# Attention of all heads by pairs in float32: scores on row halves, values on column halves, and the weights turned by VectorE and moved by DMA

## The chip, the cores and the metric

The kernel runs on one core of a Trainium2 chip. The metric is the device time of one execution, in microseconds. The core has TensorE (PE in the profile, its weight loads PEld), VectorE (DVE), ScalarE (ACT), GpSimd (POOL) and the queue of SyncE (SP), which issues nearly all DMAs here.

## What is computed

Attention over 8 batches x 8 heads, 576 positions of 64 values each, with a mask in blocks of 64; then a feed-forward layer over the 4608 tokens of width 512, with a hidden width of 2048. Inputs and outputs are float32 (the weights of the feed-forward arrive as 64-bit floats).

```python
scores = (q @ k.T) / sqrt(64)                 # per head, 576 x 576
scores = where(i // 64 >= j // 64, scores, -1e9)
attn = exp(scores - scores.max(-1)); attn /= attn.sum(-1) + 1e-9
x = concat_heads(attn @ v)                    # 4608 x 512
h = x @ w_in                                  # 4608 x 2048
out = (h * sigmoid(1.702 * h)) @ w_out        # 4608 x 512
```

## The kernel before

**Feed-forward.** The tokens are cut into 12 tiles of 384. A tile runs over 16 units, one for each 128 hidden columns. A unit is 12 matmuls of 384 columns into the PSUM tile `hp` (each factor is split in a rounded part and a remainder, `xh`/`xl` and `wih`/`wil`, and three products are summed), then tanh on ACT (L517), `g` on DVE (L518, it reads `hp`), the split into `gh` (ACT, L522) and `gl` (POOL, L81), and, one unit later, 9 matmuls of 512 columns into `acc0` to `acc2`. `hp` has one buffer: the 12 matmuls of a unit wait until DVE has made the `g` of the unit before, and only that unit's 9 `acc` matmuls of the one before stand between.

**Attention.** A head is worked in 5 chunks of query rows: chunk 0 has 64 rows, chunks 1 to 4 have 128, against 64, 192, 320, 448 and 576 keys (`width`). `score` makes the scores of a chunk into a PSUM bank and takes their largest on DVE (L313), the exponentials and their sums on ACT (L321), then scales the weights `e` by the reciprocal of the sum (L330 to L344). `fill` turns the weights by PE transposes in blocks of 128x128 against `ident` (L382) and copies them to SBUF (L386, L389); `av` multiplies them with `v`. The first 17 heads (`early`) load q and k row by row and turn them on PE, and multiply turned weights and values in float32 (`vn`). The other 47 load q and k in 32-wide slices, turn them in 32x32 blocks on DVE (L244, L248), split them and multiply by rounded part and remainder on all 128 rows (`q1`, `k1`, `q2`, `ph`, `pl`, `vs`, `vd`).

**Order.** PE runs in the order in which the program is written. `step(n)` gives the slots of a head from the strings in `ORDER`. Behind each slot the feed-forward is advanced to a share of its work that `TILES_BY` gives by position: nothing up to head 8.8, one tile from there to head 17, nine tiles over the other 48 heads, and the last two tiles after all attention. The 32 weight pieces (`weight_piece`, 64 DMAs) are converted along the way by `WEIGHTS_BY`, the last at head 15. The other engines' instructions are put in order by a scheduler within these limits. An engine works its instructions off in that order, and a waiting one holds those behind it.

**Turns of names.** `xr` holds the result of attention, turned, as a ring of two batches; `bank()` hands out PSUM banks in turn: `w0` to `w3`, and `acc0` to `acc2` as well while the first heads run.

## Time and profile before

| | |
|---|---|
| time, median of 3 runs | 1218.23 us (1216.92 to 1220.74) |
| the profiled execution | 1218.16 us, span of its instructions 1216.4 us |
| granted TensorE clock, mean | 0.994 |
| PE / PEld busy | 1188.4 us (98%) / 1063.9 us (87%) |
| DVE / ACT / POOL busy | 872.0 (72%) / 706.7 (58%) / 367.6 (30%) us |
| DMA | 78.62 MB in 223772 packets, 65 GB/s in the mean |
| chain that ended last | PE 87%, DVE 7%, ACT 2%, issue 2% |

In a row of the groups by line stand line, engine, operation, output<-inputs with their shapes, count, then busy us in all and the mean ns of one, and behind the second bar the engine's idle time before them. A float32 matmul leaves two records in the trace, one for each pass. In a row of the timeline stand start, length, engine, line and operation; rows of one kind are merged, with their count at the end. Matmuls are pipelined, so that their length says less than the distance between two starts.

### The profile page before, as it was taken

What the parts mean: (1) busy time and instruction counts of PE and PEld (TensorE: products, weight loads), DVE (VectorE), ACT (ScalarE), POOL (GpSimd) and SP (SyncE); (2) the same over time, 40 slices, a digit from 0 to 9 for tenths busy, and PEclk for the clock granted to TensorE, in tenths of its full rate; (3) what the DMA queues carried; (4) which work ended last, traced back from release to release, by engine and by line L of the source; (5) the groups of instructions that cost most, each with busy time, mean ns of one, the idle gap of its engine ahead of it and who ended that gap; (6) DMA issues with size and microseconds to landing.
All of it is one profiled execution on the core that took longest, in us unless ns stands there. A gap on an engine that the chain in (4) does not pass through costs nothing.

```text
span 1216.4 us, 20880 instructions
## 1 busy us (share of the span) xinstructions
PE 1188.4 (98%) x6860; PEld 1063.9 (87%) x6860; DVE 872.0 (72%) x2460; ACT 706.7 (58%) x1773; POOL 367.6 (30%) x496
## 2 busy tenths in 40 slices
PE   6899999999999999999999999999999999999998
PEld 5667887789999999999999999999999999999997
DVE  6997788777887888778888787878788788611111
ACT  6886666655665565656665665565575566432322
POOL 3554454421321312321322232232132231232321
PEclk8999999999999999999999999999999999999999
DMA  8653444422222231232132232222232231000000
GB/s 201 162 152 94 118 117 119 108 42 51 50 70 44 55 76 40 48 81 50 38 76 55 44 70 50 51 70 45 53 76 43 46 77 30 4 26 1 27 1 26
DMA packets 223772, 78.62 MB, mean 65 GB/s; under 512 B 198832, under 2 KB 204848, under 8 KB 223664
## 3 DMA queue, kind: packets, MB, share of 16 engines
q1 hardware_dynamic: 222480, 77.00, 27.0%
q8 instruction: 54, 0.88, 0.3%
q14 instruction: 54, 0.44, 0.1%
q10 hardware_dynamic: 1184, 0.30, 0.1%
HBM read 50.87 MB, written 9.44 MB: 50 GB/s over the span
## 4 chain that ended last, share of the span: by engine, by line
PE 87%; DVE 7%; ACT 2%; issue 2%; DMA 1%; POOL 1%; POOLq 0%; SPq 0%; DVEq 0%; ACTq 0%
PE hp L92 32%; PE acc L92 32%; PE bank L92 15%; PE bank L95 8%; DVE e L313 1%; DVE wm L171 1%; DVE wm L176 1%; ACT e L321 1%; DVE sm L330 1%; DVE wm L167 1%; DVE e L342 1%; DVE qk L286 1%; DMA wst<-in_moe_w_out_dram 0%; DMA qkr<-in_q_dram 0%; DVE xr L427 0%
## 5 line engine op out<-in xcount | busy, mean ns | idle before, releaser
L81 POOL TENSOR_TENSOR gl<-g,gh 128x384 fp32r<-128x384 f32 x192 | 197.2, 1027 | 599.5 <-ACT gh L522 521.7
L321 ACT ACTIVATE e<-e,mx 64x64 f32<-64x64 f32 (+4 forms) x320 | 180.0, 563 | 214.8 <-DVE mx L313 213.8
L92 PE MATMUL hp<-xh,wih 128*128 128x384 f32 x768 | 268.0, 349 | 2.4 <-ACT wih L180 1.9
L92 PE MATMUL hp<-xl,wih 128*128 128x384 f32 x768 | 259.6, 338 | 1.2 <-POOL sm L297 1.2
L92 PE MATMUL hp<-xh,wil 128*128 128x384 f32 x768 | 259.0, 337 | 0.9 <-POOL wil L81 0.9
L92 PE MATMUL acc<-woh,gh 128*128 128x512 f32 x576 | 237.0, 412 | 0.5 <-ACT woh L180 0.5
L92 PE MATMUL acc<-wol,gh 128*128 128x512 f32 x576 | 227.2, 395 | 0.6 <-POOL wol L81 0.6
L92 PE MATMUL acc<-woh,gl 128*128 128x512 f32 x576 | 226.7, 394 | 0.5 <-POOL gl L81 0.5
L518 DVE SCALAR_TENSOR_TENSOR g<-g,hp 128x384 f32<-128x384 f32 x192 | 105.3, 548 | 129.4 <-ACT g L517 128.3
L313 DVE CUSTOM_DVE_ANT_0 e<-bank,mask 64x64 f32<-64x64 f32 (+4 forms) x320 | 132.9, 420 | 69.3 <-PE bank L92 65.6
L517 ACT ACTIVATE g<-hp 128x384 f32<-128x384 f32 x192 | 93.9, 489 | 119.2 <-PE hp L92 115.9
L95 PE MATMUL bank<-ident,e 128*128 128x128 f32 x960 | 153.9, 280 | 8.1 <-DVE e L342 5.6
L92 PEld LDWEIGHTS hp<-xh,wih 128*128 128x128 f32 x768 | 144.6, 188 | 11.5 <-ACT wih L180 2.1
L92 PEld LDWEIGHTS hp<-xh,wil 128*128 128x128 f32 x768 | 144.9, 189 | 9.6 <-POOL wil L81 1.2
L92 PEld LDWEIGHTS hp<-xl,wih 128*128 128x128 f32 x768 | 144.3, 188 | 1.6 <-POOL sm L297 1.6
L390 DVE TENSOR_TENSOR pl<-bank,ph 128x512 fp32r<-128x512 f32 (+2 forms) x188 | 102.4, 562 | 56.7 <-ACT ph L389 56.6
L342 DVE TENSOR_SCALAR e<-e,sm 64x64 f32<-64x64 f32 (+2 forms) x260 | 137.2, 557 | 4.9
L92 PEld LDWEIGHTS acc<-wol,gh 128*128 128x128 f32 x576 | 108.3, 188 | 26.2 <-POOL wol L81 1.1
L95 PEld LDWEIGHTS bank<-ident,e 128*128 128x128 f32 x960 | 112.1, 142 | 21.1 <-DVE e L342 8.0
L522 ACT CAST gh<-g 128x384 fp32r<-128x384 f32 x192 | 97.6, 508 | 52.9 <-DVE g L518 52.2
L92 PE MATMUL bank<-qk 128*128 128x320 f32 (+4 forms) x384 | 118.3, 308 | 2.7 <-DVE qk L286 1.8
L92 PEld LDWEIGHTS acc<-woh,gh 128*128 128x128 f32 x576 | 108.7, 189 | 11.0 <-ACT woh L180 0.7
(68 smaller groups left out, 1845.4 us busy)
## 6 DMA issues: line engine op xcount, KB each, us to landing
qkd<-qkd SPq DMA_DIRECT2D x94, 144.0 KB, 2.3
out_dram<-osb SPq DMA_DIRECT2D x36, 256.0 KB, 2.1
qkd<-in_q_dram SPq DMA_DIRECT2D x94, 72.0 KB, 2.4
qkd<-in_k_dram SPq DMA_DIRECT2D x94, 72.0 KB, 2.2
vr<-in_v_dram SPq DMA_DIRECT2D x47, 128.0 KB, 2.4
wst<-in_moe_w_out_dram SPq DMA_DIRECT2D x18, 256.0 KB, 3.2
qkr<-in_q_dram SPq DMA_DIRECT2D x17, 256.0 KB, 3.4
xr<-in_moe_w_in_dram SPq DMA_DIRECT2D x16, 256.0 KB, 3.1
```

What stands on the lines that cost most here:

```text
L81: eng.tensor_tensor(out=out, in0=in0, in1=in1, op=ALU.subtract)
L92: return tc.keep_in_program_order(nc.tensor.matmul(**kw))
L95: return tc.keep_in_program_order(nc.tensor.transpose(**kw))
L167: nc.vector.tensor_scalar(out=m, in0=m, scalar1=3, scalar2=None, op0=ALU.logical_shift_left)
L171: nc.vector.scalar_tensor_tensor(out=y, in0=w[..., 1], scalar=0x80000000, in1=y, op0=ALU.bitwise_and, op1=ALU.bitwise_or,)
L313: nc.vector.tensor_tensor_reduce(out=e[0:m, lo:hi], in0=s[0:m, 0 : hi - lo], in1=mk, op0=ALU.add, op1=ALU.min, scale=-0.125, scalar=3e38 i ...
L321: nc.scalar.activation(out=e[0:m, 0:w], in_=e[0:m, 0:w], func=AF.Exp, scale=-1.0, bias=mx[0:m, i : i + 1], accum_out=sm[0:m, i : i + 1],)
L342: nc.vector.tensor_scalar(out=x, in0=x, scalar1=sc, scalar2=None, op0=ALU.mult)
L390: nc.vector.tensor_tensor(out=lo, in0=tp[:, 0:tot], in1=f(hi), op=ALU.subtract)
L517: nc.scalar.activation(out=g, in_=hp[:, 0:tt], func=AF.Tanh, scale=1.702)
L518: nc.vector.scalar_tensor_tensor(out=g, in0=g, scalar=1.0, in1=hp[:, 0:tt], op0=ALU.add, op1=ALU.mult)
L522: nc.scalar.copy(out=gh, in_=g)
```

## The change

Attention is worked in 32 pairs of heads (`NPAIR`), all in one way.

- **Loads.** 8 DMAs bring q and k of both heads in 32-wide slices, head 0 on partitions 0 to 63, head 1 on 64 to 127 (`raw`); two DVE transposes turn them (`prep`, now L210). 4 DMAs bring the values (`vp`). No split and no second copy of anything is made. `raw`, `qk`, `vp` have one buffer each.
- **Scores.** One float32 matmul per chunk and head (two in chunk 4, for 256 and 320 keys), over 64 rows of the array: head 0 on rows 0 to 63, head 1 on rows 64 to 127, one behind the other, each into its own bank.
- **Weights.** They are scaled as before (by POOL, but for chunk 4, and in the first pairs chunk 0, by DVE or ACT: `SCALE_ON`), then turned by DVE in 32x32 blocks into `tw` (L282, L287 of the changed kernel), and behind chunk 4 of a pair 16 DMAs (L294) bring the blocks to their places in `pw`. `tw` and `pw` have one buffer each, and `e` one for even chunks and one for odd ones.
- **Values.** Float32 matmuls of 64 output columns: head 0 writes partitions 0 to 63 of the bank, head 1 partitions 64 to 127, one behind the other; two ACT copies then bring both heads to `xr`.
- **Order.** `01`, `23` and `4` stand for the scores of these chunks of pair n, `V` for the values of pair n-1, `L` for turning q and k of pair n+1 and loading those of n+2; behind each slot the feed-forward advances as before.
- **Weight pieces** are converted in halves, each with a buffer of its own.

```diff
-    "S0+F2 S1+F3 F4 S2 A S3 S4 F1+S5 B",
+    "01 - 23 - V 4 L -",
+    "01 - - - 23 - - V - 4 - - L - - -",
+    "01 - - - 23 - - V - 4 - - L - - -",
...
-TILES_BY = ((8.8, 0), (17, 1), (65, -2))
+TILES_BY = ((9, 0), (17, 1), (65, -2))
...
+    NS = 14
+    SLOT = (None, 0, 1, 3, 6)
+    turned = sp.tile([P, 8 * NS - 4, 2, 32], F32, name="turned")
+    tw, pw = [
+        turned[:, x : x + 4 * NS].rearrange("p (b s) h c -> p b s h c", b=4) for x in (0, 4 * NS - 4)
+    ]
...
+    def score(n, chunks):
...
+        for i in chunks:
+            a, z = qrange(i)
+            w = width(i)
+            for lo, hi in ((0, w),) if w <= 512 else ((0, 256), (256, w)):
+                for hd in range(2):
+                    s = bank()
+                    r = slice(hd * D, hd * D + D)
+                    mm(
+                        out=s[0 : z - a, 0 : hi - lo], lhsT=qk[n][r, 0, a:z], rhs=qk[n][r, 1, lo:hi],
+                        start=True, stop=True,
+                    )
+                    todo.append((i, hd, lo, hi, s))
+        e = {}
+        for i, hd, lo, hi, s in todo:
+            e[i] = weigh(n, i, hd, lo, hi, s, e.get(i))
+        for i in chunks:
+            turn(n, i, e[i])
...
+    def turn(n, i, e):
...
+        on = SCALE_ON[phase(n)][i]
+        for hd in range(2):
...
+            if i:
+                nc.vector.transpose(
+                    out=tw[:, :, SLOT[i] : SLOT[i] + i, hd].rearrange("p b j c -> p j b c"),
+                    in_=e[:, hd, 0 : i * P],
+                )
+        r = slice(BLK, P) if i else slice(0, BLK)
+        nc.vector.transpose(
+            out=tw[r, 0:2, 9 + max(i, 1)].rearrange("p b h c -> p h b c"), in_=e[r, :, i * P : w]
+        )
+        if i == NCH - 1:
+            for kb in range(4):
+                for qb in range(4):
+                    ns = 10 if kb > 1 else NS if qb > 1 else 11
+                    nc.sync.dma_start(
+                        out=pw[kb * 32 : kb * 32 + 32, qb, 0:ns], in_=tw[qb * 32 : qb * 32 + 32, kb, 0:ns]
+                    )
+
+    def av(n):
...
+        for x, (bk, c, nn, j, w) in enumerate(todo):
+            for hd in range(2):
+                mm(
+                    out=bk[hd * D : hd * D + D, c : c + nn].rearrange("d (a c) -> d a c", c=32),
+                    lhsT=vp[:, hd, j], rhs=w[:, :, hd], start=x in (0, last + 1), stop=x >= last,
+                )
```

What this does to the order is shown at one place of the stage in which 24 pairs pass beside nine tiles: the end of a pair's scores. On PE, before, the last scores of a head (`bank<-qk_9253` with 256 columns is the first part of chunk 4) stand among pieces of a unit:

```order
L92 MATMUL hp<-xl,wih 128x384
L92 MATMUL bank<-qk_9253 128x256
L92 MATMUL bank<-qk_9253,q_9254 128x256
L92 MATMUL acc_8728<-woh,gh 128x512
L92 MATMUL acc_8728<-woh,gl 128x512
L92 MATMUL acc_8728<-wol,gh 128x512
```

Now all four matmuls of chunk 4, two for each part, stand between the `acc` matmuls of one unit and the `hp` matmuls of the next:

```order
L83 MATMUL acc_5945<-wol,gh 128x512
L83 MATMUL bank<-qk 128x256 x2
L83 MATMUL bank<-qk 128x320 x2
L83 MATMUL hp<-xh,wih 128x384
L83 MATMUL hp<-xh,wil 128x384
```

What moved: the scores of two heads stand as one piece, and no transposes follow them. On DVE, before, a `g` of the feed-forward (L518) stands between the two parts of chunk 4, ahead of its scaling (`e_88` is chunk 4):

```order
L313 ISA e_88,mx<-bank,mask 128x256
L313 ISA mx 128x1
L330 TENSOR_SCALAR sm<-sm 128x1
L518 SCALAR_TENSOR_TENSOR g<-g,hp 128x384
L333 RECIPROCAL sm<-sm 128x1
L342 TENSOR_SCALAR e_86<-e_86,sm 128x448
L313 ISA e_88,mx<-bank,mask,mx 128x320
L313 ISA mx 128x1
```

Now the next `g` (L403) stands behind the last maximum of chunk 4, a transpose of `prep`, the reciprocal, the scaling and the three transposes of the weights:

```order
L249 ISA e,mx<-bank,mask,mx 128x320
L249 ISA mx 128x1
L210 STREAM_TRANSPOSE qk<-raw 128x576
L268 TENSOR_SCALAR sm<-sm 128x2
L271 RECIPROCAL sm<-sm 128x2
L278 TENSOR_SCALAR e<-e,sm 128x576 x2
L282 STREAM_TRANSPOSE turned<-e 128x4x4x32 x2
L287 STREAM_TRANSPOSE turned<-e 64x2x2x32
L403 SCALAR_TENSOR_TENSOR g<-g,hp 128x384
```

What moved: that `g` belongs to the unit whose `hp` matmuls stand right behind chunk 4 on PE, and the unit after it waits for it.

More of the change, by code (lines that the diff above doesn't have):

```diff
@@ L174, in weight_piece @@
             )
-        for w, y in halves:
             nc.vector.scalar_tensor_tensor(
@@ L189, in convert, with heads @@
             conv["n"] += 1
[L192 removed]
+    raw, qk = {}, {}
+    def heads(n):
+        b, h = divmod(n, HP)
+        return [(hd, b, 2 * h + hd) for hd in range(2)]
     def load(n):
[L195 to L212 removed]
+        raw[n] = d2.tile([P, 2, S // 32, 32], F32, tag="raw", name="raw", bufs=1)
+        for x, src in enumerate((q, k)):
+            for hd, b, h in heads(n):
@@ new lines, in load_v @@
+    def load_v(n):
+        for hd, b, h in heads(n):
+            nc.sync.dma_start(
+                out=vp[:, hd, 0:QC], in_=v[b, h, 0 : QC * P].rearrange("(c p) d -> p c d", p=P)
+            )
+            nc.sync.dma_start(out=vp[0:BLK, hd, QC], in_=v[b, h, QC * P : S])
+    def prep(n):
+        qk[n] = d2.tile([P, 2, S], F32, tag="qk", name="qk", bufs=1)
+        for x in range(2):
+            nc.vector.transpose(out=qk[n][:, x], in_=raw[n][:, x].rearrange("p c d -> p (c d)"))
+        raw.pop(n)
@@ L303, in score @@
         w = width(i)
-        e = es[i]
-        s = bank()
-        for qq, st in ((q1, True), (q2, False)):
-            mm(
-                out=s[0:m, 0 : hi - lo], lhsT=qq[:, a:z], rhs=k1[:, lo:hi],
-                start=st, stop=not st,
-            )
+        if e is None:
+            e = d2.tile([P, 2, w], F32, tag=f"e{i % 2}", name="e", bufs=1)
         last = i > 0 and hi == w
@@ L449, in step, with item @@
-        for ci in range(6):
-            items[f"S{ci}"] = on(now, score, n, ci)
-        return [[items[y] for y in x.split("+")] for x in ORDER[phase(n)].split()]
+        now = n < NPAIR
+        def item(x):
+            if x == "V":
+                return (lambda: av(n - 1)) if n else None
+            if x == "L":
+                return (lambda: (prep(n + 1), load(n + 2) if n + 2 < NPAIR else None)) if n + 1 < NPAIR else None
+            return (lambda: score(n, [int(y) for y in x])) if now and x != "-" else None
@@ L454, in attention_moe_kernel @@
+        return [item(x) for x in ORDER[phase(n)].split()]
     done = {"split": 0}
```

323 lines of the change are left out of this document (72 added, 251 removed), and 2 rows, old and new, of the table ORDER.

## The prediction

> **What bounds the kernel now.** I read the page's first part, then busy time by stretches, then the timeline of PE and the groups by line and shape.
>
> ```profile
> PE 1188.4 (98%) x6860; PEld 1063.9 (87%) x6860; DVE 872.0 (72%) x2460; ACT 706.7 (58%) x1773; POOL 367.6 (30%) x496
> ```
>
> The same by stretches (us, PE, PEld, DVE, ACT, POOL busy, granted clock, DMA share, GB/s), cut at the first `hp`, at the end of head 15 and at the end of attention:
>
> ```profile
> 0.00:92.00 92.00, 76.06 (x457) 57.59 (x457) 78.27 (x275) 73.60 (x209) 42.99 (x66) 0.96 0.66 171
> 92.00:231.00 139.00, 132.15 (x740) 106.75 (x740) 106.53 (x319) 92.39 (x240) 71.03 (x72) 0.98 0.42 110
> 231.00:1073.00 842.00, 840.92 (x4975) 774.46 (x4974) 668.50 (x1834) 500.87 (x1246) 214.13 (x320) 1.00 0.25 54
> 1073.00:1216.40 143.40, 139.26 (x694) 125.10 (x692) 18.68 (x34) 39.84 (x80) 39.43 (x40) 1.00 0.05 17
> ```
>
> PE never rests in the third stretch: what the change is worth there is what it takes from PE, less any wait that it brings. The cuts come from these timeline rows:
>
> ```profile
> 92.29 0.42 PE L92 MATMUL hp<-xh,wih 128*128 128x384 f32 x1
> ...
> 231.23 0.37 ACT L427 COPY xr<-bank 64x256 f32<-64x256 f32 x1
> ```
>
> The third stretch holds 48 heads, 24 pairs at 842 / 24 = 35.1 us. The `hp` instructions in it are 1728 matmuls, 144 units, 6 a pair. What a unit costs alone is read after attention:
>
> ```profile
> 231.00:1073.00 842.00, 355.13 (x1728) 305.52 (x1728) 78.29 (x143) 70.22 (x144) 1.00 0.25 54
> ...
> 1100.00:1150.00 50.00, 50.00 (x253) 45.30 (x251) 6.46 (x12) 15.30 (x31) 16.04 (x16) 1.00 0.05 17
> ```
>
> 253 matmuls of 21 a unit in 50 us are 4.15 us a unit, so 6 units are 24.9 us, and attention, with all it does to PE's flow, costs 35.1 - 24.9 = 10.2 us a pair. That is the number to beat.
>
> **PE's part of a pair.** It removes everything in the 10.2 (30 transposes, split scores, split values, the joints between them) and adds float32 matmuls: per head 1600 columns of scores (64 + 192 + 320 + 448 + 576) and as many of values, 6400 a pair. The early heads of before show such matmuls:
>
> ```profile
> 128.50 0.40 PE L92 MATMUL acc<-wol,gh 128*128 128x512 f32 x1
> 128.83 2.09 PE L92 MATMUL bank<-ph,vn 128*64 128x256 f32 x10
> 130.85 0.50 PE L92 MATMUL acc<-woh,gh 128*128 128x512 f32 x1
> 131.19 0.39 PE L92 MATMUL acc<-woh,gl 128*128 128x512 f32 x1
> 131.41 0.39 PE L92 MATMUL acc<-wol,gh 128*128 128x512 f32 x1
> ```
>
> Five matmuls (3 x 256 + 192 + 64 = 1024 columns, ten records) take 130.85 - 128.83 = 2.02 us. An `acc` matmul starts 0.22 us after another (131.41 - 131.19), but 0.33 and 0.34 us pass where float32 of another shape begins or ends: 0.1 us for each change. Less two such changes (the last matmul has 64 rows), a column costs (2.02 - 0.2) / 1024 = 1.78 ns. The Trainium skill, TensorEngine Tiling (Array Packing), section Tiling Modes, says that changing the tiling mode drains TensorE, which speaks against a kernel that goes to and fro; the trace agrees with its 0.1 us. A pair has four pieces (01, 23, V, 4), eight changes, 0.8 us.
>
> One after the other, 6400 columns cost 11.4 us, with the changes 12.2. But the two heads' matmuls, issued side by side, share no rows of the array (scores) or no columns (values). Were they to run two at a time, the columns cost 5.7 us. They are issued pass by pass, both passes of head 0 before those of head 1, so at the seams a pass stands without partner; I put 1.0 us for that (an estimate: one pass of each of 64 to 448 columns at 0.89 ns). That gives 7.5 us. The bounds are 5.9 (no such seams, changes mostly hidden) and 12.2. No row of before has two matmuls on different halves, so nothing there decides between 7.5 and 12.2; I take 7.5, as the operands leave no reason to wait and PE already works its loads and matmuls at once (87% and 98% busy). The same page and section says that different tiles can execute LdWeights and Matmul in parallel; no run so far shows it. By it the sum is the one below, without it that of rival B.
>
> **The wait that it adds.** `hp` has one buffer, and PE waited for `g` practically never:
>
> ```profile
> L92 PE MATMUL hp<-xh,wih 128*128 128x384 f32 x768 | 268.0, 349 | 2.4 <-ACT wih L180 1.9 <-DVE g L518 0.5
> ```
>
> Now, once a pair, the `g` of the unit behind chunk 4 stands on DVE behind chunk 4's whole softmax and turning. PE needs it one unit, 4.15 us, after chunk 4. The durations of that chain, from the groups by shape:
>
> ```profile
> L313 DVE CUSTOM_DVE_ANT_0 e<-bank,mask,mx 128x320 f32<-128x320 f32 x64 | 35.1, 549 | 11.4 <-PE bank L92 10.9
> L321 ACT ACTIVATE e<-e,mx 128x576 f32<-128x576 f32 x64 | 49.8, 777 | 5.2 <-DVE mx L313 5.0
> L321 ACT ACTIVATION_READ_ACCUMULATOR e<-e,mx 128x1 f32 x256 | 48.0, 188 | 0.0
> L330 DVE TENSOR_SCALAR sm<-sm 128x1 f32<-128x1 f32 x128 | 18.8, 147 | 5.2 <-ACT e L321 5.0
> L342 DVE TENSOR_SCALAR e<-e,sm 128x576 f32<-128x576 f32 x56 | 29.6, 529 | 1.6
> L244 DVE STREAM_TRANSPOSE tmp<-qkd 128x576 f32<-128x576 f32 x47 | 36.0, 765 | 0.5 <-DVE sm L330 0.4
> L518 DVE SCALAR_TENSOR_TENSOR g<-g,hp 128x384 f32<-128x384 f32 x192 | 105.3, 548 | 129.4 <-ACT g L517 128.3
> ```
>
> The first head's maximum (0.55) and exponential (0.78 + 0.19), then the second's (0.97), end at 2.5 us; `prep`'s transpose fits in beside them. Then 2 x 0.147 for the reciprocal, 2 x 0.529 for the scaling, two transposes of 512 columns at 765 / 576 ns (1.36), one of 64 (0.28 with its start), and `g` (0.55): 6.0 us, with some 0.3 for signals 6.3. So PE waits 6.3 - 4.15 = 2.2 us. Bounds: 1.2 (instructions that follow each other overlap at their ends) and 3.6 (transposes with scattered output cost double). Another `g`, behind chunk 2's turn, waits for POOL's scaling; 0.4 us for it (0 to 0.8). DVE itself loses work (no subtractions, no unpacking of transposes), ACT too; both are idle enough to be no bound.
>
> A pair then takes 24.9 + 7.5 + 2.2 + 0.4 = 35.0 us, against 35.1: over 24 pairs -2 us. The gain on PE and the wait cancel.
>
> **The 16 DMAs and the opening.** From the issue rows of SP and the landings:
>
> ```profile
> 609.43 1.16 SPq L230 DMA_DIRECT2D vr<-in_v_dram  x2
> ...
> qkd<-qkd SPq DMA_DIRECT2D x94, 144.0 KB, 2.3
> ```
>
> An issue takes 0.58 us and a landing 2.3, so 16 take 16 x 0.58 + 2.3 = 11.6 us. In the third stretch they have from behind chunk 4 to the next V, 14 of 16 slots, some 28 us: hidden. In the first four pairs nothing hides them, and the single `tw` and `e` buffers chain one pair to the next. Until they have landed, DVE cannot turn chunk 1 of the next pair, and the maxima of chunk 3 and all of chunk 4 stand behind that:
>
> ```profile
> L313 DVE CUSTOM_DVE_ANT_0 e<-bank,mask 128x448 f32<-128x448 f32 x64 | 39.8, 622 | 17.7 <-PE bank L92 17.4
> L313 DVE CUSTOM_DVE_ANT_0 e<-bank,mask 128x256 f32<-128x256 f32 x64 | 26.9, 420 | 27.2 <-PE bank L92 27.2
> L321 ACT ACTIVATE e<-e,mx 128x448 f32<-128x448 f32 x64 | 42.8, 668 | 108.0 <-DVE mx L313 107.8
> L340 POOL TENSOR_TENSOR e<-e,sm 128x448 f32<-128x448 f32 x17 | 16.1, 945 | 4.3 <-PE bank L92 2.3 <-DVE sm L333 2.0
> L171 DVE SCALAR_TENSOR_TENSOR wm<-wst,wm 128x256 uint32<-128x256 uint32 x34 | 16.4, 520 | 0.3
> ```
>
> Turns of chunks 1 and 2 (0.9), maxima of chunk 3 (1.24), the second exponential (0.86), reciprocal (0.3), scaling on POOL (1.89), its turn (0.8), maxima of chunk 4 (2 x 0.42 + 2 x 0.55, 2.0), exponentials (1.3), reciprocal and scaling (1.4), turns (1.7): 12.4 us, with the DMAs 24. I take 24.5. The first values can start when 8 loads (8 x 0.58 + 2.3), two transposes (1.5), the chunks through two `e` buffers (some 18, from the same rows) and 16 DMAs (11.6) are through: 38 us. Three more pairs make 111, and V itself brings the first `hp` to some 115, against 92. The next four pairs have one tile beside them: PE has 16.6 + 7.5 us of work, but the chain is 24.5 + 4 x 0.55 for `g` and some 5 of the 10 us that converting 17 pieces puts on DVE a pair (17 pieces x 2 halves x about 1.25 us / 4): 31.7. So the values of pair 7 end at 115 + 4 x 31.7 = 242, say 243, against 231: +12 us. Bounds: -20 (22 and 28 us a pair) and +30, as weight loads now stand between the 16 in SP's queue and have waited up to 6.9 us:
>
> ```profile
> SPq L159 <- DVE wm L176: 53.9, 23, 6.9
> ```
>
> **The sum.** Opening +12, third stretch -2, the last two tiles as before: 1216.4 + 12 - 2 = 1226.4 us of span, and 1.8 around it as in the profiled execution (1218.16, against a median of 1218.23): 1228 us.
>
> **The rivals.**
> A, the forecast: 1212 to 1265 by the bounds of the wait (24 x -1.0 or +1.4) and the opening. Chance 0.50.
> B, slower: the halves do not run at once. A pair's columns cost 12.2 instead of 7.5; the wait falls by about 0.9, since the first scores come earlier against the last. 24 x (4.7 - 0.9) = 91, and 2 a pair for the first four: 1228 + 91 + 8, about 1327. If only scores or only values overlap, half of it: 1280. For it: no row shows overlap, and matmuls on the same rows and columns come strictly in turn. Against: disjoint operands. It decides from about 8 us a pair. Chance 0.23.
> C, faster: the passes pair up without seams and PE's part is 5.9 us. 24 x -1.6 = -38: 1190; with the wait at its lower bound 1166. For it: loads of weights already run beside matmuls; against: eight changes of shape at 0.1 us that the trace shows. It decides where PE's part and its waits together fall under 9.5 us a pair (10.2, less 12 / 24 for the opening, less 0.2 for the margin). Chance 0.27.
>
> **How the numbers follow.** About 0.3% (3.7 us) is what a measurement here can tell from no change. Faster: C's 0.27 and 0.08 of A, 0.35. Same: 0.06 of A. Slower: 0.36 of A and B's 0.23, 0.59. The range, 1172 to 1320, leaves out the upper half of B and the lower end of C; A's own range is 1212 to 1265.
>
> **What would show it.** Starts of the scores' passes: head 1's passes starting before head 0's have run out (right), or strictly 0.89 ns a column apart (B). Idle time of PE before the unit behind chunk 4, released by `g`: about 2 us a pair; under 0.5 makes the wait wrong. The first `hp` at about 115 us and the end of pair 7 at 243. 35 us a pair after that; 39 is B, 33.4 C. A wait of PE's V for the 16 DMAs in the third stretch would make the forecast wrong on a point that I hold for settled.

## The result, and the profile after

| | before | changed kernel |
|---|---|---|
| time, median | 1218.56 us (1216.92 to 1220.74, 4 runs) | 1278.79 us (1278.37 to 1280.93, 4 runs) |
| ratio to before | | 1.0497, 95% interval 1.0476 to 1.0517 |
| span of the profiled execution | 1216.4 us | 1279.1 us |
| granted TensorE clock, mean | 0.994 | 0.924 |
| forecast | | 1228 us, 1172 to 1320 |

The kernel got 5.0% slower where 0.8% was forecast. The page's first part, and busy time by the same stretches as before (stretch, length, then PE, PEld, DVE, ACT, POOL busy with the number of records, granted clock, DMA share, GB/s), cut at the first `hp`, at the end of pair 7's values, and at the end of attention:

```profile
PE 1093.9 (86%) x6720; PEld 908.0 (71%) x6720; DVE 627.4 (49%) x2008; ACT 497.6 (39%) x1325; POOL 437.9 (34%) x552
```

```profile
0.00:128.30 128.30, 49.33 (x353) 36.04 (x353) 81.52 (x280) 53.95 (x160) 37.17 (x56) 0.61 0.52 120
128.30:295.60 167.30, 118.87 (x655) 89.35 (x654) 117.17 (x338) 74.92 (x211) 70.17 (x90) 0.80 0.50 128
295.60:1136.30 840.70, 787.11 (x5027) 658.03 (x5025) 411.01 (x1358) 328.79 (x876) 293.11 (x371) 0.98 0.34 76
1136.30:1279.10 142.80, 138.56 (x690) 124.55 (x690) 17.74 (x32) 39.94 (x80) 37.44 (x37) 1.00 0.05 17
```

All of it was lost in the first two stretches. The opening ends at 295.6 us where it ended at 231.2: +64.4. The third stretch takes 840.7 against 842, the tail 142.8 against 143.4. PE, which was busy for 208 of the first 231 us, is now busy for 168 of 296, and its granted clock there is 0.61 and 0.80.

How a pair of the opening runs is read from PE's timeline (start, length, operation, and in brackets the idle time ahead and what ended it), here from the values of pair 1 to those of pair 2:

```profile
61.41 5.60 PE L83 MATMUL bank<-turned,vp 128*64 128x128 f32 x60 [6.64 <-DMA turned<-turned]
66.94 1.24 PE L83 MATMUL bank<-qk 64*128 64x256 f32 x8
74.52 3.98 PE L83 MATMUL bank<-qk 64*64 64x64 f32 x16 [6.33 <-DVE qk L210]
93.48 0.80 PE L83 MATMUL bank<-turned,vp 128*64 128x128 f32 x6 [14.99 <-DMA turned<-turned]
```

and, for the 15 us of waiting at its end, from DVE's last turned block and SP's queue behind it:

```profile
73.34 0.31 DVE L287 STREAM_TRANSPOSE turned<-e 64x128 f32<-64x128 f32 x1
```

```profile
76.74 2.29 SPq L150 DMA_DIRECT2D xr<-in_moe_w_out_dram  x2
79.08 0.50 SPq L204 DMA_DIRECT2D vp<-in_v_dram  x1
79.68 1.83 SPq L150 DMA_DIRECT2D xr<-in_moe_w_in_dram  x2
81.57 10.06 SPq L294 DMA_DIRECT2D turned<-turned  x16
```

The pair is a closed loop: what ends one turn must happen before the next can start. From the landing of the transfers to the last turned block it takes from 61.4 to 73.65. Two paths run side by side in the first half of that, the values on PE and chunk 3's softmax and turning on DVE, ACT and POOL, and they are of nearly one length: DVE had turned chunk 3 at 67.46 and then waited 0.22 us for chunk 4's scores.

```profile
67.68 0.42 DVE L249 CUSTOM_DVE_ANT_0 e<-bank,mask 128x256 f32<-128x256 f32 x1 [0.22 <-PE bank L83]
```

Then the 16 transfers should go, but SP stands at weight loads until 81.57, 7.9 us later; they take 10.1 us to issue and 1.5 more to land, and only then come the next values. From the values of pair 0 to those of pair 1, with no weight load in the way, it is 24.2 us; here 32.1.

In pairs 4 to 7 the feed-forward's first tile runs beside attention, and there PE also stands still for weights that are not converted yet. Its waits from 122.7 to 295.6 us (engine, tile and line, what it waited for: total, times, longest), on the copies that make `wih`, `woh` and `wil`:

```profile
PE hp L83 <- ACT wih L169: 17.4, 5, 10.7
PE acc L83 <- ACT woh L169: 7.4, 1, 7.4
PE hp L83 <- POOL wil L72: 2.6, 5, 1.2
```

Together 27.4 us, of which 24.9 fall between the values of pair 5 and those of pair 6, which are 63.3 us apart (198.46 and 261.73).

Starts of the values, read from PE's timeline of each run, tell how far the opening has come. The last column is the ratio to the kernel before, with its 95% interval. Some runs don't do the whole work: e5, e10, e17 and e18 convert only 16 of 256 columns fully, e6 keeps no remainder of the output weights, e13 and e16 to e18 move blocks to wrong places, and e12 multiplies by the weights of the wrong pair.

| run | values of pair 3 | pair 7 | pair 8 | time, us | ratio |
|---|---|---|---|---|---|
| changed kernel | 122.7 | 292.6 | 341.1 | 1278.8 | 1.050 (1.048 to 1.052) |
| e1 weight loads by ACT | 171.3 | 286.2 | 324.7 | 1265.7 | 1.041 (1.039 to 1.043) |
| e2 weight loads by POOL | 196.9 | 308.3 | 347.1 | 1287.7 | 1.059 (1.057 to 1.062) |
| e3 16 transfers by ACT | 132.7 | 303.4 | 340.8 | 1278.9 | 1.051 (1.049 to 1.053) |
| e4 8 by ACT, 8 by SP | 123.1 | 296.0 | 342.4 | 1279.5 | 1.052 (1.049 to 1.054) |
| e5 thin conversion | 120.1 | 275.9 | 323.0 | 1263.9 | 1.037 (1.036 to 1.039) |
| e6 two turned buffers | 122.2 | 281.6 | 332.0 | 1382.7 | 1.133 (1.131 to 1.135) |
| e7 even conversion | 142.3 | 270.5 | 309.0 | 1248.7 | 1.025 (1.023 to 1.027) |
| e8 values serial | 130.6 | 310.3 | 352.2 | 1350.7 | 1.109 (1.107 to 1.110) |
| e9 even, by POOL | 162.1 | 318.6 | 359.8 | 1298.2 | 1.067 (1.066 to 1.069) |
| e10 even and thin | 138.6 | 268.9 | 311.3 | 1247.7 | 1.025 (1.023 to 1.028) |
| e11 two hp banks | 122.9 | 292.7 | 342.0 | 1289.3 | 1.059 (1.057 to 1.061) |
| e12 even, chunk 4 first | 156.8 | 296.9 | 335.4 | 1277.9 | 1.051 (1.049 to 1.052) |
| e13 four transfers | 113.5 | 274.3 | 321.3 | 1261.6 | 1.036 (1.034 to 1.039) |
| e14 transfers kept together | 154.3 | 279.3 | 317.7 | 1258.0 | 1.033 (1.031 to 1.035) |
| e15 values behind chunk 4 | 154.2 | 288.5 | 327.3 | 1265.0 | 1.039 (1.037 to 1.042) |
| e16 kept together and four | 132.5 | 277.9 | 316.3 | 1253.5 | 1.030 (1.027 to 1.031) |
| e17 thin and four | 111.4 | 263.5 | 309.1 | 1252.0 | 1.028 (1.026 to 1.029) |
| e18 even, thin and four | 133.1 | 261.2 | 302.2 | 1240.5 | 1.018 (1.017 to 1.020) |

### The profile page after: what moved, and what is told of

The parts are those of the page before. It is cut to its first block, busy times and chain, and to the rows that moved or that the text cites. A ratio compares the mean times of both kernels' runs of the same rounds, so it can differ in the third digit from the quotient of the medians.

```text
span 1279.1 us, 19933 instructions
## 1 busy us (share of the span) xinstructions
PE 1093.9 (86%) x6720; PEld 908.0 (71%) x6720; DVE 627.4 (49%) x2008; ACT 497.6 (39%) x1325; POOL 437.9 (34%) x552
## 5 line engine op out<-in xcount | busy, mean ns | idle before, releaser
L83 PE MATMUL hp<-xh,wih 128*128 128x384 f32 x768 | 276.9, 361 | 76.8 <-DVE g L403 59.2
L83 PE MATMUL hp<-xh,wil 128*128 128x384 f32 x768 | 265.7, 346 | 3.5 <-POOL wil L72 2.6
L83 PE MATMUL hp<-xl,wih 128*128 128x384 f32 x768 | 264.1, 344 | 1.4 <-POOL xl L72 1.4
L83 PE MATMUL acc<-woh,gh 128*128 128x512 f32 x576 | 232.3, 403 | 17.4 <-ACT woh L169 17.4
L403 DVE SCALAR_TENSOR_TENSOR g<-g,hp 128x384 f32<-128x384 f32 x192 | 106.3, 554 | 268.5 <-ACT g L402 266.8
L249 DVE CUSTOM_DVE_ANT_0 e<-bank,mask 64x64 f32<-64x64 f32 (+4 forms) x320 | 122.8, 415 | 161.9 <-PE bank L83 160.8
L276 POOL TENSOR_TENSOR e<-e,sm 128x320 f32<-128x320 f32 (+3 forms) x240 | 146.9, 634 | 160.8 <-DVE sm L271 142.6
L83 PE MATMUL bank<-qk 64*128 64x320 f32 (+4 forms) x768 | 130.5, 450 | 41.1 <-DVE qk L210 39.7
L282 DVE STREAM_TRANSPOSE turned<-e 128x128 f32<-128x128 f32 (+3 forms) x256 | 119.6, 495 | 56.7 <-POOL e L276 47.6
L83 PE MATMUL bank<-turned,vp 128*64 128x128 f32 (+1 forms) x1920 | 108.6, 277 | 40.7 <-DMA turned<-turned 37.8
L83 PEld LDWEIGHTS bank<-turned,vp 128*64 128x64 f32 x1920 | 104.2, 151 | 53.9 <-issue 50.4
```

The lines of the kernel that those rows point to most:

```text
L83: return tc.keep_in_program_order(nc.tensor.matmul(**kw))
L249: nc.vector.tensor_tensor_reduce(out=e[0:m, hd, lo:hi], in0=s[0:m, 0 : hi - lo], in1=mk, op0=ALU.add, op1=ALU.min, scale=-0.125, scalar=3e ...
L276: nc.gpsimd.tensor_tensor(out=x, in0=x, in1=sc.to_broadcast([m, w]), op=ALU.mult)
L282: nc.vector.transpose(out=tw[:, :, SLOT[i] : SLOT[i] + i, hd].rearrange("p b j c -> p j b c"), in_=e[:, hd, 0 : i * P],)
L403: nc.vector.scalar_tensor_tensor(out=g, in0=g, scalar=1.0, in1=hp[:, 0:tt], op0=ALU.add, op1=ALU.mult)
```

## The experiments

### Other queues: e1 to e4

The first theory was SP's queue: by the trace it is 7.9, 5.4, 5.7, 10.2 and 11.9 us in pairs 2 to 6 by which the 16 transfers start late or stretch beyond 10.1 us, 41 us together.

```diff
-            d = nc.sync.dma_start(out=w, in_=src[:, a : a + 1])
+            d = nc.scalar.dma_start(out=w, in_=src[:, a : a + 1])    # e1; e2: nc.gpsimd
```

> The weight loads are issued from ACT's queue, the 16 transfers of a pair stay on SP's. Theory Q (queue): in the changed kernel the 16 transfers of pairs 2 to 6 stand behind or between weight loads that wait in SP's queue for a staging buffer, which costs 7.9, 5.4, 5.7, 10.2 and 11.9 us (start of issue after the last turned block, and issue beyond 10.1 us), together 41 us, and because one buffer of turned weights serves all pairs, the next pair's turning waits for them. Freed of that, issue starts at the last turned block in every pair and takes 10.1 us, the values of pair 7 start near 251 instead of 293, and the time is 1238 (1228 to 1248). Theory D (DVE): conversion, softmax and turning on DVE set the pace of the opening, whatever queue the loads go through: the values of pair 7 stay at 285 to 295, time 1270 to 1285. Theory I (issue): the 10.1 us of issue and 1.5 of landing of a pair are what costs: no change either.

> The weight loads are issued from POOL's queue instead of SP's. Theory Q: the same 41 us as with ACT's queue, 1238, less what POOL loses by standing at loads that wait for staging, since it scales chunks 1 to 3 of the exponentials (1238 to 1255). Theories D and I: no change, 1270 to 1285.

```diff
-                    nc.sync.dma_start(
+                    (nc.scalar if n < 2 * HP else nc.sync).dma_start(    # e3
+                    (nc.scalar if n < 2 * HP and qb % 2 else nc.sync).dma_start(    # e4
```

> The 16 transfers of pairs 0 to 7 are issued from ACT's queue, the weight loads stay on SP's. Theory Q: as in the kernel with the weight loads on ACT, about 41 us are gained, less up to 10 us in a pair where ACT's exponentials and copies stand behind the 16 issues: 1238 to 1260, and the issue starts at the last turned block. Theory D: 1270 to 1290, since ACT only gets more to do. Theory I: issue takes as long on ACT as on SP, no gain: 1275 to 1290.

> Of the 16 transfers of pairs 0 to 7 eight go through ACT's queue and eight stay on SP's. Theory I: issue falls from 10.1 to 5.0 us a pair, the first pairs follow at 19 us instead of 24, 7 x 5 us = 35 us are gained: 1244. Theory Q: pairs 0 and 1 gain 5 us each, but in pairs 2 to 6 the eight on SP's queue still wait behind weight loads for most of the 41 us: 1255 to 1270. Theory D: 1270 to 1285.

The theory that the queue alone costs 41 us fell: -13, +9, 0 and +1 us instead of -41. The cleanest of the four is e2: there SP issued the 16 of every pair of the opening in 10.1 to 11.2 us, and the kernel was slower all the same, with POOL now standing at the loads. In e1 the work only moved. Its stretches from the values of pair 0 to those of pair 3, and on to pair 7 (columns as above):

```profile
44.90:171.30 126.40, 32.58 (x252) 23.43 (x253) 110.26 (x309) 66.36 (x186) 57.50 (x76) 0.58 0.61 160
171.30:286.20 114.90, 99.49 (x655) 80.55 (x655) 65.53 (x223) 46.17 (x135) 38.50 (x48) 0.94 0.40 85
```

With the loads free to run ahead, nearly all conversion fell into pairs 0 to 3, where DVE was then busy 87% and a pair took 42 us. Pairs 4 to 7, left almost without conversion, took 114.9 us, 28.7 each, with the feed-forward's four units in them: 35.5 for the first, which still held two half pieces and a wait of 13.5 us for the transfers, and 26.5 each for the other three. That is near the price of those pairs themselves. In the pairs with conversion the transfers did not get faster; SP needed up to 19.1 us for 16 of them, here 18.4:

```profile
67.50 18.38 SPq L294 DMA_DIRECT2D turned<-turned  x16
```

In e3 and e4 ACT stood at the issues (11.4 us for 16 in pair 2 of e3), and its next exponential came only behind them.

### What DVE has to do with it, and the second buffer: e5 and e6

```diff
-                out=y, in0=y, scalar1=3, scalar2=None, op0=ALU.logical_shift_left
+                out=y[..., 0:16], in0=y[..., 0:16], scalar1=3, scalar2=None, op0=ALU.logical_shift_left
```

and the same in the two steps behind it (e5).

> The three DVE steps of each half weight piece work on 16 of its 256 columns (the rest of the converted weights is then not the reference's); the order of all instructions stays. The four runs before gave 1266 to 1288 whatever queue the loads or the 16 transfers went through, so theory Q is out. Theory D (DVE): the 64 halves take 1.43 us each of DVE now and some 0.25 then, 75 us less, and since DVE is 81 to 88% busy in pairs 2 to 6 nearly all of that comes off the opening: the values of pair 7 start near 225 to 235 instead of 293 and the time is 1210 to 1222. Theory C (chain): turning, 16 transfers and the next turning follow each other in 24 us a pair, and PE then waits for ACT's and POOL's part of the conversion; DVE's steps are hidden in that: less than 25 us come off, 1255 to 1275.

-15 us. The three steps of a half piece, by their medians (min/median/max in ns), of the changed kernel and then of e5:

```profile
L158 DVE TENSOR_SCALAR wm<-wm x64: 279/286/880, 27.1 to 307.5; 128x256 uint32<-128x256 uint32 x64
L161 DVE SCALAR_TENSOR_TENSOR wm<-wst,wm x36: 410/424/1246, 182.1 to 308.1; 128x256 uint32<-128x256 uint32 x36
L165 DVE SCALAR_TENSOR_TENSOR wm<-wst,wm x36: 382/426/841, 183.3 to 308.6; 128x256 uint32<-128x256 uint32 x36
```

```profile
L158 DVE TENSOR_SCALAR wm<-wm x64: 159/175/765, 27.2 to 289.8; 128x16 uint32<-128x16 uint32 x64
L161 DVE SCALAR_TENSOR_TENSOR wm<-wst,wm x36: 165/175/658, 176.8 to 290.0; 128x16 uint32<-128x16 uint32 x36
L165 DVE SCALAR_TENSOR_TENSOR wm<-wst,wm x36: 131/175/887, 177.5 to 290.2; 128x16 uint32<-128x16 uint32 x36
```

So 1.14 us became 0.53, not 0.25 as I had put it, and 64 x 0.61 = 39 us of DVE's time went; 15 came off the end. DVE's time is part of the cause and not the whole.

```diff
+    tw0, pw, tw1 = [ ... for x in (0, 4 * NS - 4, 8 * NS - 4) ]
...
+        tw = (tw0, tw1)[n % 2]
-                for gi, (ga, wb) in enumerate(((g_hi, woh), (g_lo, woh), (g_hi, wol))):
+                for gi, (ga, wb) in enumerate(((g_hi, woh), (g_lo, woh), (g_hi, woh))):
```

> Two buffers of turned weights, used in turn, so that the next pair's turning needn't wait for the 16 transfers; to make room the low half of the output weights isn't kept, and PE reads the high half twice in its place, in as many passes. Theory C: the loop of 12.3 us of turning and 11.9 us of transfers opens; pairs 0 to 3 follow at 17 to 19 us plus 1.43 a half piece, the opening gets 35 us shorter or more: 1230 to 1245. Theory D: DVE has the same work, and the profile puts down only some 6 us of its waits to the 16 transfers: 1268 to 1279.

In the opening 9 us came off up to pair 8, and pairs 0 to 3 kept their pace (values of pair 3 at 122.2 against 122.7): the second buffer alone does not open the loop. The rest of the run was 113 us longer, which neither theory had. The longest of PE's waits of e6 from pair 8 on (total, times, longest) and of DVE's from 600 to 1000 us:

```profile
PE hp L83 <- DVE g L404: 109.9, 45, 3.7
```

```profile
DVE g L404 <- ACT g L403: 97.2, 20, 9.1
```

In the order that DVE got with the second buffer it stands up to 9.1 us at a `g` whose unit PE has not finished, with the softmax behind it. Why the scheduler put it there was not followed up.

### Conversion spread evenly: e7, e9, e10

```diff
-WEIGHTS_BY = ((0, 0), (9, 30), (15, 64))
+WEIGHTS_BY = ((0, 0), (15, 64))
...
-            d = nc.sync.dma_start(out=w, in_=src[:, a : a + 1])
-            if j < 3:
-                tc.keep_in_program_order(d)
+            d = nc.scalar.dma_start(out=w, in_=src[:, a : a + 1])    # e9: nc.gpsimd
+            tc.keep_in_program_order(d)
```

> The weight loads go through ACT's queue, all in program order, and fall due evenly from pair 0 to pair 7 (a straight line to all 32 pieces), so that DVE's order holds 8 to 12 half pieces a pair instead of 0, 8, 8, 8, 10, 21, 7. Theory D: a pair of the opening is then the longer of the 24.2 us loop and DVE's 16.9 + 1.43 a half with a tenth of stalls, 30 us at 8 halves, 36 at 12; the values of pair 7 start near 250 and PE no longer waits for late weights: 1222 to 1240. Theory C: a pair costs its loop plus the conversion, 24.2 + 1.43 x 8 = 36 us, 37 + 7 x 36 = 289 at pair 7, no gain: 1265 to 1282.

e7 is the fastest version that leaves nothing out: -30 us, and still 2.5% over the kernel before. PE no longer waited for late weights (27.4 us in the changed kernel, none here), but by the trace SP's transfers now waited for loads to land that ACT had issued (waits of SP's queue):

```profile
SPq L293 <- DMA xr<-in_moe_w_in_dram: 16.7, 12, 3.8
SPq L293 <- DMA wst<-in_moe_w_in_dram: 12.1, 5, 3.4
SPq L293 <- DMA wst<-in_moe_w_out_dram: 8.4, 4, 3.0
```

That is 37 us, and the 16 took 13.6 to 18.3 us to issue in pairs 0 to 6. And DVE seemed to be the bound, 89 to 93% busy in most pairs. So both were taken away, one at a time.

> As the kernel with even conversion (1248.7), but the weight loads go through POOL's queue instead of ACT's. There SP's 16 transfers waited 37 us in all for weight loads to land, although these were issued by ACT, and a pair's issue took 13.6 to 18.3 us instead of 10.1. Theory Q (transfers held up by weight loads): with POOL's queue the issue is back at 10.1 us, each pair of the opening is 4 to 5 us shorter, the values of pair 7 start at 235 to 245 instead of 270: 1215 to 1225. Theory D (DVE's time): DVE is 89 to 93% busy there already, the pairs stay at 30 to 32 us: 1240 to 1255, POOL's stands at loads included.

> As the kernel with even conversion (1248.7), with DVE's three steps of each half piece on 16 of its 256 columns (the converted weights are then not the reference's). Theory D: DVE's three steps take 0.53 us instead of 1.13 by their medians, 64 x 0.6 = 38 us less in an opening where DVE is 90% busy: the values of pair 7 start near 235 and the time is 1210 to 1220. Theory Q: the 16 transfers still wait for weight loads to land, and only 5 to 15 us come off: 1234 to 1244.

Neither helped. e9 had its issue back at 10.1 to 10.7 us and lost 50; PE waited for DVE's maxima as it had not in e7 (e9's waits of PE from 30 to 340 us):

```profile
PE bank L83 <- DVE mx L248: 45.2, 13, 11.1
```

e10 gained 1 us, which its runs (1243 to 1251) cannot tell from nothing. The stretches from the values of pair 0 to those of pair 7, of e7 and then of e10, show that DVE (third pair of numbers) had not been the bound at all:

```profile
47.60:270.50 222.90, 135.07 (x908) 109.26 (x909) 167.25 (x525) 111.33 (x319) 94.01 (x120) 0.77 0.54 135
```

```profile
45.80:268.90 223.10, 132.95 (x908) 106.67 (x908) 142.97 (x527) 110.13 (x318) 90.58 (x121) 0.79 0.55 136
```

It was busy for 167 of 223 us, 75%. The 89 to 93% of the expectations, and the 81 to 88% of e5's, were sums of record lengths, and DVE's records overlap at their ends: a misreading of mine. With 24 us less on DVE the same seven distances take the same 223 us.

### The steady stage: e8 and e11

```diff
-        for x, (bk, c, nn, j, w) in enumerate(todo):
-            for hd in range(2):
+        for hd in range(2):
+            for x, (bk, c, nn, j, w) in enumerate(todo):
```

> The value passes of the two heads follow each other, all of the first head's and then all of the second's, instead of alternating. If the column halves run side by side only because passes of both heads alternate (starts 54 ns apart for 128 columns where one alone takes 107), each pair's values get longer by the 40 passes of 128 columns x 53 ns + 20 of 64 x 27 ns = 2.7 us; 23 pairs in the steady stage, where PE is the bound, add 61 us, the opening little: 1335 to 1350. If pairs of halves overlap whatever the order (queue looks ahead), 1279.

+72 us, just above what was expected. The values of one pair in the steady stage, in the changed kernel and in e8:

```profile
477.88 2.98 PE L83 MATMUL bank<-turned,vp 128*64 128x128 f32 x60
```

```profile
687.30 5.57 PE L83 MATMUL bank<-turned,vp 128*64 128x128 f32 x60
```

The same 60 passes take 2.98 us when the heads alternate and 5.57 when they do not. So here two halves of the array run at a time, and PE did not reach past 30 passes of the one head for a partner of the other.

```diff
-                hp = ps.tile([P, 512], F32, tag="h", name="hp")
+                hp = ps.tile([P, 512], F32, tag=("h", "w3")[fc % 2], name="hp")
...
-        tags = ["w0", "w1", "w2", "w3"] + ...
+        tags = ["w0", "w1", "w2"] + ...
```

> hp alternates between two banks; scores and values have three banks instead of four behind the first eight pairs' start. It tests the wait of 2.2 us a pair in the steady stage. If that wait is what stands between units and nothing follows it, 23 pairs x 1.6 to 2.2 us come off: 1228 to 1242. If three banks make PE wait for DVE's maxima (chunk 4 alone needs four), each pair gets 1 to 3 us longer instead: 1290 to 1345.

+10 us. Two groups of PE from 600 to 1000 us (count, then busy us, mean ns, idle time ahead), in the changed kernel and in e11:

```profile
L83 PE MATMUL hp<-xh,wih 128*128 128x384 f32 x278 | 98.9, 356 | 19.2 <-DVE g L403 19.2
L83 PE MATMUL bank<-qk 64*128 64x320 f32 (+4 forms) x280 | 42.7, 415 | 0.0
```

```profile
L83 PE MATMUL hp<-xh,wih 128*128 128x384 f32 x276 | 96.2, 349 | 0.0
L83 PE MATMUL bank<-qk 64*128 64x320 f32 (+4 forms) x278 | 65.1, 422 | 0.0
```

The whole wait for `g`, 19.2 us, is gone. But with three banks the scores keep PE busy for 22.4 us more at almost the same mean length (422 against 415 ns), so that the two heads' scores overlap less. That a second head waits for a bank is the likely reason; the profile shows no such wait by itself. The wait for `g` was real, and the bank that removes it was worth as much where it stood.

### The loop: e12 to e18

What was left was the loop itself. e12 starts from e7:

```diff
-    "01 - 23 - V 4 L -",
+    "01 - 23 - 4 L V -",
```

> As the kernel with even conversion (1248.7), with chunk 4 and the next pair's preparation ahead of the previous pair's values in the first four pairs. Theory L (loop): in the changed kernel the values of a pair stand in PE's order ahead of the next pair's chunk 4, whose turned blocks the next 16 transfers need, so that transfers, values, chunk 4 and transfers follow each other; with chunk 4 ahead the first four pairs get 4 to 7 us shorter each: 1222 to 1235. Theory D: DVE is the bound there (85 to 92% busy): 1242 to 1255.

This run (1277.9 us) does not test it: the edit also put the 16 transfers ahead of the previous pair's values, which then read the next pair's turned weights and waited for them (PE's waits for the transfers are 90.3 us up to 300 us, 31.0 the longest). e15 does what e12 meant. In e13 the transfers themselves are cut:

```diff
+            if n < 2 * HP:
+                for o, i4 in (
+                    (pw[0:BLK, :, 0:10], tw[0:BLK, :, 0:10]),
+                    (pw[BLK:P, :, 0:10], tw[BLK:P, :, 0:10]),
+                    (pw[0:BLK, 2:4, 10:NS], tw[BLK:P, 0:2, 10:NS]),
+                    (pw[0:BLK, 0:2, 10:11], tw[0:BLK, 0:2, 10:11]),
+                ):
+                    nc.sync.dma_start(out=o, in_=i4)
+                return
```

> The changed kernel, but in pairs 0 to 7 the turned blocks are moved by 4 transfers of nearly the same bytes in place of 16 (blocks then lie in wrong places, so that the values of these pairs are not the reference's). Theory L (loop): transfers, values, the next chunk 4 and the next transfers follow each other in a pair of the opening, 12.3 us of work and 10.1 + 1.5 us of transfers; with 2.5 us of issue the pairs without conversion follow at about 17 us instead of 24, every pair of the opening gets some 7 us shorter, and 8 pairs give 50 to 60: 1220 to 1232. Theory D (conversion, late weights and PE's own units bound the opening): the time freed is filled by waits for ACT, POOL and late weights, 1255 to 1272.

-17 us, within the range of theory D and a third of what theory L said. SP's timeline of e13 tells why:

```profile
46.54 6.51 SPq L298 DMA_DIRECT2D turned<-turned  x4
```

Four transfers of the same bytes take 6.5 us to issue, 1.6 each in the mean, not four times 0.63; the values start 1.9 us behind the last issue, as they do behind 16. The issue got 10.1 - 6.5 = 3.6 us shorter, and the values of pair 1 follow those of pair 0 in 20.9 us instead of 24.2. Of a pair without conversion, then, nearly all that is taken from the transfers comes off, as a loop would have it.

e14 keeps the 16 of a pair and the weight loads each in program order on SP's queue (`tc.keep_in_program_order` around both, `WEIGHTS_BY = ((0, 6), (13, 64))`). e15 has the same (with `((0, 4), (14, 64))`) and moves the 16 into an item `M` of their own in the first four pairs:

```diff
-    "01 - 23 - V 4 L -",
+    "01 - 23 - 4 V M L",
```

> The changed kernel with all loads on SP's queue, the 16 transfers of a pair and the weight loads each kept in program order, and the pieces due by a straight line from 3 at the start to all 32 at pair 6.5. The 16 then follow each other without a load between, and DVE's order holds 14, 10, 4, 16, 8, 3, 5, 4 half pieces a pair. Theory L with the queue as part of it: issue is 10.1 us in every pair, the 41 us that loads between the transfers cost are mostly gone, and no weight comes late: the values of pair 7 start near 250 and the time is 1222 to 1240. If the loads only move the wait (SP stands at a load for a staging buffer ahead of the 16): 1250 to 1270.

> As the kernel with the transfers kept together, pieces due from 2 at the start to 32 at pair 7, and in the first four pairs chunk 4 stands ahead of the previous pair's values and the 16 transfers behind them. Theory L: PE no longer waits for the transfers ahead of chunk 4; from landing to the last turned block it is 8 us instead of 12.4, and PE's 6 us of values run beside chunk 4's softmax: 4 us a pair less in four pairs than without it, 15 us in all: 1208 to 1228. Without a loop over the values: the same as the kernel with the transfers kept together, within 8 us.

> The kernel with the transfers kept together and 4 transfers in place of 16 in pairs 0 to 7 (values of these pairs not the reference's). Theory L: another 5 to 7 us a pair come off that kernel until DVE (17 us + 1.1 a half piece) is the bound: 35 to 50 us less than it, 1180 to 1200. Theory D: less than 15 us less than it.

e14 brought 21 us. Its issue is 10.1 us in every pair, but now the wait stands ahead of the 16, as SP holds them behind loads that wait for a staging buffer (where a raw half piece lies until it is converted); in pair 0 the last turned block was there at 25.7:

```profile
37.18 4.39 SPq L150 DMA_DIRECT2D xr<-in_moe_w_in_dram  x4
41.63 10.11 SPq L293 DMA_DIRECT2D turned<-turned  x16
```

e15 was 7 us slower than e14. The only pair without conversion and without a held queue took 21.8 us instead of 24.2, but in pairs 0, 1, 3 and 5 the 16 stood 15.9, 9.3, 23.9 and 17.5 us behind loads. The move gives something where nothing else stands in the way. e16 gained 4 us on e14, not 35 to 50.

> The changed kernel with both cuts at once: DVE's three conversion steps on 16 of 256 columns, and 4 transfers in place of 16 in pairs 0 to 7 (converted weights and the values of these pairs are then not the reference's). Alone they brought 15 and 17 us. If the two costs stand one behind the other in the opening, they add up: 1245 to 1250. If DVE and the transfers take each other's place as the bound (one waits while the other works), together they bring clearly more than their sum: 1215 to 1235. If a third cost holds the opening (weight loads in SP's queue and weights that come late for PE), less than the sum: 1250 to 1262.

> The same two cuts in the kernel with even conversion over ACT's queue (1248.7; with DVE's cut alone 1247.7). If the parts only add up, the transfers' cut brings 17 us here too: 1228 to 1234. If DVE, the transfers and the queue take each other's place, all three cut together bring the opening back to the 24 us or less of a pair that holds no conversion: the values of pair 8 start at 255 to 280 instead of 341, 1195 to 1218. If a further cost holds it: 1238 to 1248.

e17: -27, where the parts alone gave 15 + 17 = 32. They nearly add, so neither hides the other, and the 5 us that are missing put it in the range named for a third cost. One that neither cut touches is seen in its trace: between the values of pairs 5 and 6 PE still waits 22 us for late weights, and these are 59 us apart. e18: all three cuts, -38, and still 23 us over the kernel before; the transfers' cut brought 7 us here (1247.7 to 1240.5). Its longest waits of PE from 35 to 262 us:

```profile
PE bank L83 <- DVE qk L209: 35.8, 3, 12.6
PE bank L83 <- DVE mx L248: 16.5, 4, 9.7
PE hp L83 <- DVE g L411: 15.7, 8, 5.6
PE bank L83 <- DMA raw<-in_q_dram: 11.3, 2, 6.4
```

What PE then waits for is the next pair's q and k, 47 us in the first and the last of these rows. They are turned on DVE behind chunk 4, and their loads (L193) stand in SP's queue until weight loads have landed, by the trace, though ACT issued those. Three of SP's waits from 20 to 310 us:

```profile
SPq L193 <- DMA xr<-in_moe_w_out_dram: 14.7, 4, 5.7
SPq L193 <- DMA wst<-in_moe_w_out_dram: 12.5, 7, 3.9
SPq L193 <- DMA wst<-in_moe_w_in_dram: 12.3, 5, 4.6
```

That is 39.5 us. No run takes these waits away alone, and what holds the rest of the opening stays open.

## Why the prediction was wrong

**The step that failed** is the term for the conversion of the weights in the opening. The prediction gave it "some 5 of the 10 us that converting 17 pieces puts on DVE a pair", 20 us in pairs 4 to 7, and nothing in pairs 0 to 3. What the opening costs without conversion can be put together from runs: first values at 37.2, three pairs of 24.2 (pair 1, which has no conversion), and the 114.9 us of e1's pairs 4 to 7: 224.7 for the values of pair 7. The changed kernel has them at 292.6. So conversion, with all that comes with it, cost 68 us for the 60 half pieces that were done by then, 1.1 us each, where 20 were forecast; 48 of the 52.6 us by which the end of pair 7 came later than forecast (295.6 instead of 243). This is put together from distances in two runs; no run leaves conversion out altogether.

The reasoning behind the 20 was that most of DVE's work fits into DVE's idle time. In the kernel before it did: PE had 208 us of work in 231, and the conversion lay beside it. In the changed kernel PE's work is gone from the opening, and a pair is a chain of latencies over PE, DVE, ACT, POOL and SP's queue. What is put on several of them lengthens it: DVE's steps (e5: 15 us for 39 of DVE's time), SP's loads ahead of and between the 16 (41 us by the trace, but a gain of 13 alone), late weights. The prediction saw the loop and priced it well (24.5 us a pair; measured 24.2, with 12.3 from landing to the last turned block where 12.4 were forecast), named the loads between the 16 as a bound of +30, and then added half of DVE's conversion time in pairs 4 to 7 and nothing else for conversion.

Where the 68 us show on PE can be read from the rows above. In pairs 0 to 3 it is 13 us, SP's holds of 7.9 and 5.4. From the first `hp` to the end of pair 7's values PE works off 655 records, as many as in e1's second stretch, and of the 52 us that it takes longer (167.3 against 114.9), 27 are the waits for late weights and 19 are PE's own busy time, 118.9 against 99.5, at a granted clock of 0.80 against 0.94. The rest is some 6 us. That is a sum of what PE did, not of causes: a slower PE ahead of a wait costs nothing.

Which share belongs to which engine is shown only in part: taking away DVE's steps gave 15 us, shortening the transfers' issue by 3.6 us a pair 17, placement and queue together 30 (e7), all three 38. That the queue alone is the cause fell (e2 above all), that DVE's time alone is fell too (e5, e10), and so did the second buffer (e6).

**PE's part of a pair**, 7.5 us with overlapping halves: right. Two starts of values in the steady stage:

```profile
686.73 1.54 PE L83 MATMUL bank<-turned,vp 128*64 128x128 f32 x27
...
720.84 1.33 PE L83 MATMUL bank<-turned,vp 128*64 128x128 f32 x24
```

This pair is 34.1 us; less 24.9 for the units and 1.8 for the wait, 7.4 are left. e8 shows rival B's price for the values alone, 72 us (11 of them in the opening), where half of B had been put at 52. The Trainium skill, TensorEngine Tiling (Array Packing), section Tiling Modes, says that different tiles can execute LdWeights and Matmul in parallel; the trace agrees where the heads alternate, by 2.98 against 5.57 us.

**The wait for `g`**, 2.2 us a pair: right in kind and near in size, in the third stretch 42.2 / 23 = 1.8 us. It came once a pair: the second wait, put at 0.4 us, does not show. Nothing on PE there waited for the 16 transfers:

```profile
PE hp L83 <- DVE g L403: 42.2, 23, 3.2
PE acc L83 <- ACT woh L169: 10.0, 1, 10.0
PE hp L83 <- POOL xl L72: 1.4, 2, 0.7
```

That it cancels PE's gain: right, 840.7 / 24 = 35.03 us a pair, forecast 35.0. That the figures meet so closely is luck in part: the usual pair takes 34.1 us, and the mean is raised by a first distance of 48.5 us (values of pair 7 to pair 8), with one wait of 10 us for late weights, and by some of 36 to 38. **The 16 DMAs**: 10.1 + 1.5 = 11.6 us, as forecast; hidden in the steady stage, as forecast. **The first values**: 37.2 us, forecast 38. **The first `hp`**: 128.3, forecast 115; SP's holds in pairs 2 and 3 (7.9 and 5.4) are as long as that difference.

The range held the time (1172 to 1320), and slower was the likelier side. But that the range held is luck: 1278.8 us lies above what A, the forecast, was given (1212 to 1265), and the range reached further only for B, whose mechanism did not occur. The way it got slower was none of the rivals: the upper bound of the opening's term, +30, was less than half of the 64.4 measured. Its lower bound does not follow from its own figures either: pairs of 22 and 28 us in place of 24.5 and 31.7 take off 3 x 2.5 + 4 x 3.7 = 22 us, which makes -10 of the +12, not -20.

## What to carry to other kernels

Work that a busy engine hides is free only as long as that engine is the bound: before taking work from it in a stage, draw the loop that is left (what must end before the next turn can start, on every engine and queue), and ask of all that stands in any of those queues whether it adds to its length, rather than count what remains after idle time is filled. In such a loop no single engine need look full (DVE was busy for 13.1 of the 24.2 us of the pair without conversion), and a queue that holds short urgent transfers should not also hold loads that wait for buffers. Here two halves of the array ran together only where the program alternated them, and a bank taken from there to remove another wait cost as much as it gave.

## What the runs showed that was not expected

- **The clock in the emptied opening.** The 60 value passes of a pair take 5.60 us at 61.41 us, where the granted clock is 0.50 (0.61 over the whole stretch), and 2.98 us in the steady stage at 1.00. The kernel before had 0.96 in its first stretch. The Trainium skill, TensorE: Matmul & The Clock Gate, Part 1, says that the array runs at half its clock unless it has lately been busy; the trace agrees. In the loop of 24.2 us these 2.6 us cost little, since DVE's path beside the values left PE only 0.22 us behind. In pairs 4 to 7 PE's 19 us more of busy time may cost more; no run here kept PE busy to test it.
- **Queues that are not independent.** By the trace the 16 transfers on SP waited 37 us for loads issued by ACT to land (e7), and SP's loads of q and k 39.5 us in e18. With the loads on POOL, 16 transfers were issued in 10.1 to 11.2 us (e2). Why a queue waits for the other's loads is not shown.
- **Issue does not go by count.** 16 transfers of 32 partitions take 10.1 us to issue, 4 with the same bytes 6.5.
- **Loads on POOL's queue** cost 9 us instead of gaining 41 (e2), and 50 more than on ACT's (e9).
